# Batch 0 of a frequency filter and two-layer network on pairs of PSUM banks instead of single ones

## The chip, the cores and the metric

The kernel runs on one core of a Trainium2 chip. The metric is device time in microseconds (us) of one execution. Single executions of one kernel spread, so small differences are read in two ways: from the times of several executions, as a ratio with a 95% interval, and from milestones inside a trace of one execution.

## The reference, cut to what matters

```python
# x: 8 batches x 3008 positions x 256 channels; filters: 1505 frequencies x 256
Y = np.fft.rfft(x, axis=1) * (filt_r + 1j * filt_i)[None]
y = np.fft.irfft(Y, n=3008, axis=1).reshape(8 * 3008, 256)
h = y @ w_in                                   # 256 -> 2048
out = (0.5 * h * (1 + erf(h / sqrt(2)))) @ w_out   # 2048 -> 256
```

The two large products are 78% of the chain that ended last in the kernel before (41% and 37%). The Fourier transform is done as small products with cosine and sine tables, 3008 = 47 x 64.

## The kernel before: the parts that matter

The transforms of batches 1 to 7 run inside the slots of the main loop, beside the large products, and go through memory between their stages. Batch 0 has nothing to hide behind. It stays on the chip and alternates small products with transposes:

- `c1`: first forward stage, 8 groups, as the columns of x land; `c1t` transposes it into `b_sb`.
- `c2`: second forward stage and, on VectorE, its product with the filters `F` (real and imaginary). There are twelve of these, "products 0 to 11". The filters arrive in four transfers, and the last brings what products 8 to 11 need.
- `c3`: first inverse stage into `vt`, six copies of two halves on ScalarE.
- `c3t` and `s4`: transpose and last inverse stage into `y`, from which the first large product reads.

Everything passes through PSUM, which the kernel takes as eight banks of 512 fp32 columns. Before, each stage takes single banks in rotation:

```python
def bank(self, name, wide=False):
    pools = {"f": self.ps_f, "h": self.ps_h, "o": self.ps_o}   # 3, 3 and 2 banks
    tag = "f"
    if wide:
        tag = "fhofhofh"[self.turn % 8]
        self.turn += 1
    return pools[tag].tile([128, 512], FP32, tag=tag, name=name)

def c2(self, p):
    p1, p2 = (self.pp.tile([128, 512], BF16, tag=t, name=t) for t in ("p1", "p2"))
    for t, o, n in ((p1, 1, 0), (p2, 0, 1)):
        ps = self.bank("ps_c2", True)
        ...                                     # two matmuls of 256 columns
        nc.vector.tensor_tensor(out=t, in0=ps, op=ALU.mult, in1=F[:, n, ...])

# main part, before the loop over the large products
for u in range(16): m.c1(u // 2, u % 2)         # one half of a group each
m.tables_inverse()                              # T4, T4c and T3, before the filter stage
for p in range(14):
    if p < 12: m.c1t(p)
    if 1 <= p < 13: m.c2(p - 1)
    if p in (3, 5, 7, 9, 11, 13): m.c3((p - 3) // 2)
for u in range(20):
    if u < 16: m.c3t(u)
    if u >= 3 and u % 2 == 1 and (u - 3) // 2 < 8:
        for h in range(2): m.s4(0, (u - 3) // 2, h, both=True)
```

## Time and profile before

| | before |
|---|---|
| time, median of 4 (lowest to highest) | 791.66 us (790.64 to 792.34) |
| span of the profiled execution | 790.6 us |
| TensorE busy | 762.5 us, 96% |
| second half of product 8 starts | 35.26 us |
| last `vt` copy ends | 41.04 us |
| first w_in product | 50.20 us |
| first w_out product | 60.43 us |

Up to the first w_in product it is batch 0's own speed that counts, and from there on TensorE is busy nearly all the time (729.7 of 740.4 us). So a microsecond gained or lost before 50.2 should show at the end. In the stretch from the last `vt` copy to the first w_in product the groups by form are, on VectorE and ScalarE (name of the line, engine, operation, what it writes and reads, shapes, count, busy us and mean ns, idle before):

```profile
L218 DVE CAST d_sb<-ps_c3t 96x512 bf16<-96x512 f32 x8 | 5.3, 678 | 2.2 <-PE ps_c3t L383 2.2
...
L216 ACT ACTIVATE d_sb<-ps_c3t 96x512 bf16<-96x512 f32 x8 | 4.7, 595 | 0.4 <-PE ps_c3t L383 0.4
L220 DVE TENSOR_SCALAR y_sb<-ps_s 128x376 bf16<-128x376 f32 x8 | 4.3, 538 | 0.1
L216 ACT ACTIVATE y_sb<-ps_s 128x376 bf16<-128x376 f32 x8 | 3.9, 486 | 1.0 <-PE ps_s L306 0.8
```

Both engines copy both stages evenly and VectorE hardly idles once it has begun.

### The profile page before, as it was taken

Reading aid. Unit: us, or ns where it says so; the run is one execution under the profiler, and the core shown is the slowest. Engines: PE = TensorE matmul, PEld = TensorE weight load, DVE = VectorE, ACT = ScalarE, POOL = GpSimd, SP = SyncE. Lnnn points to the kernel's source line nnn. Section 1 sums busy time; section 2 is a strip of 40 time slices with the busy share of each in tenths; the row PEclk is TensorE's granted clock in tenths of the full one; section 3 lists DMA queues with packets and bytes.
Section 4 is the critical chain, followed back from the end, with each engine's and each line's share of the span. In section 5 each row is a group of like instructions: output and inputs, shape, how many; then the busy total and the mean of one; then the engine's idle time right before and its main releaser. Section 6 shows DMA issues by size and latency. Waiting matters only on the chain.

```text
span 790.6 us, 14618 instructions
## 1 busy us (share of the span) xinstructions
PE 762.5 (96%) x5817; PEld 539.1 (68%) x5914; DVE 407.6 (52%) x733; ACT 570.5 (72%) x982; POOL 65.3 (8%) x161
## 2 busy tenths in 40 slices
PE   4799999999999999999999999999999999999997
PEld 4556776677676767667677676667767767666666
DVE  7784756466464645646455564546645366411011
ACT  6688965798557885588755887569865688666663
POOL 8610200011000200002000010001100000000000
PEclk9999999999999999999999999999999999999999
DMA  8994862555435553446614566154642521401111
GB/s 128 178 161 132 158 161 68 147 119 114 114 84 155 104 135 84 109 139 130 145 50 109 148 119 157 40 160 108 125 130 65 162 78 58 133 31 38 41 41 54
DMA packets 88390, 87.21 MB, mean 110 GB/s; under 512 B 6081, under 2 KB 78273, under 8 KB 88321
## 3 DMA queue, kind: packets, MB, share of 16 engines
q1 hardware_dynamic: 77760, 68.70, 30.6%
q0 software_dynamic: 10560, 17.57, 15.5%
q8 instruction: 46, 0.75, 0.4%
q14 instruction: 24, 0.19, 0.1%
HBM read 57.15 MB, written 46.66 MB: 131 GB/s over the span
## 4 chain that ended last, share of the span: by engine, by line
PE 90%; DMA 5%; DVE 2%; POOL 1%; issue 1%; ACT 0%; SPq 0%; DVEq 0%; POOLq 0%
PE ps_o L420 41%; PE ps_h L406 37%; PE ps_s L231 3%; PE ps_s L306 3%; PE ps_s L278 2%; PE ps_s L254 2%; DMA d_sb<-R 1%; DMA F<-in_filt_i_dram 1%; DMA F<-in_filt_r_dram 1%; DMA x_sb<-in_x_dram 1%; DVE d_sb L218 1%; POOL x_sb L87 1%; POOL F L95 1%; DMA R<-a_sb 1%; DMA b_sb<-R 0%
## 5 line engine op out<-in xcount | busy, mean ns | idle before, releaser
L409 ACT ACTIVATE g_sb<-ps_h 128x512 bf16<-128x512 f32 x752 | 439.4, 597 | 189.1 <-PE ps_h L406 163.5
L420 PE MATMUL ps_o<-w_out_sb,g_sb 128*128 128x256 bf16 x3008 | 449.0, 272 | 3.0
L406 PE MATMUL ps_h<-y_sb,w_in_sb 128*128 128x512 bf16 (+2 forms) x1503 | 426.6, 365 | 0.2 <-ACT y_sb L216 0.2
L420 PEld LDWEIGHTS <-g_sb 128*128 128x128 bf16 x3008 | 287.6, 98 | 133.7
L406 PEld LDWEIGHTS <-w_in_sb 128*128 128x128 bf16 x1600 | 155.1, 98 | 23.0 <-issue 0.5
L424 DVE COPY ost<-ps_o 128x512 f32<-128x512 f32 x94 | 64.4, 685 | 125.1 <-PE ps_o L420 124.6
L261 DVE TENSOR_TENSOR p<-ps_s,F 128x512 bf16<-128x512 f32 x84 | 58.1, 692 | 103.8 <-ACT p L260 97.3
L220 DVE TENSOR_SCALAR y_sb<-ps_s 128x376 bf16<-128x376 f32 x120 | 65.3, 548 | 82.0 <-PE ps_s L306 81.9
L218 DVE CAST a_sb<-ps_s 96x512 bf16<-96x512 f32 x112 | 76.3, 685 | 40.5 <-PE ps_s L231 40.4
L218 DVE CAST v_sb<-ps_s 128x512 bf16<-128x512 f32 x84 | 57.6, 687 | 12.9 <-PE ps_s L278 12.7
L306 PEld LDWEIGHTS <-d_sb 96*128 96x128 bf16 x512 | 33.8, 97 | 30.2 <-issue 2.3
L259 ACT ACTIVATE p<-ps_s 64x512 bf16<-64x512 f32 x84 | 49.9, 594 | 2.2 <-ACT g_sb L409 0.2
L260 ACT CAST p<-ps_s 64x512 bf16<-64x512 f32 x84 | 48.5, 577 | 1.0
L100 POOL COPY gate<-p 1x1 bf16<-1x1 bf16 x48 | 8.5, 176 | 480.6 <-DVE p L263 480.6
L231 PE MATMUL ps_s<-x_sb,T 94*96 94x512 bf16 x112 | 42.6, 381 | 0.5
L306 PE MATMUL ps_s<-T,d_sb 96*128 96x94 bf16 x448 | 36.3, 204 | 2.6 <-DMA d_sb<-R 1.3
L263 DVE TENSOR_TENSOR p<-p,p 128x512 bf16<-128x512 bf16 x84 | 35.7, 425 | 2.9
L87 POOL DMA_DIRECT2D x_sb<-in_x_dram x64 | 33.9, 530 | 19.0 <-issue 11.1
L262 DVE TENSOR_TENSOR p<-p,F 128x512 bf16<-128x512 bf16 x84 | 34.9, 415 | 0.0
L254 PE MATMUL ps_s<-b_sb,T 128*128 128x256 bf16 x168 | 32.1, 273 | 0.3
L278 PE MATMUL ps_s<-p,T 128*128 128x256 bf16 x168 | 32.1, 273 | 0.3
L278 PEld LDWEIGHTS <-T 128*128 128x128 bf16 x168 | 16.4, 98 | 20.1 <-DVE p L263 0.5
(84 smaller groups left out, 189.0 us busy)
## 6 DMA issues: line engine op xcount, KB each, us to landing
out_dram<-ost SPq DMA_DIRECT2D x94, 256.0 KB, 2.5
x_sb<-in_x_dram POOLq DMA_DIRECT2D x64, 188.0 KB, 3.9
R<-a_sb SPq DMA_DIRECT2D x56, 192.0 KB, 3.0
b_sb<-R SPq DMA_DIRECT2D x28, 384.0 KB, 4.4
R<-v_sb SPq DMA_DIRECT2D x42, 256.0 KB, 4.0
d_sb<-R SPq DMA_DIRECT2D x56, 192.0 KB, 4.6
w_in_sb<-in_moe_w_in_dram POOLq DMA_DIRECT2D x2, 512.0 KB, 8.6
w_out_sb<-in_moe_w_out_dram POOLq DMA_DIRECT2D x2, 512.0 KB, 10.1
```

Source lines behind the costliest of these rows:

```text
L218: self.nc.vector.tensor_copy(out=out, in_=in_)
L220: self.nc.vector.tensor_scalar(out=out, in0=in_, scalar1=scale, scalar2=None, op0=ALU.mult)
L231: nc.tensor.matmul(ps[0:96, :], lhsT=self.T1, rhs=self.st[b, "x"][:, 2 * u:2 * u + 2, :], start=True, stop=True)
L259: nc.scalar.activation(out=p2[0:64], in_=ps[64:128], func=AF.Copy, scale=-1.0)
L260: nc.scalar.copy(out=p2[64:128], in_=ps[0:64])
L261: nc.vector.tensor_tensor(out=p1, in0=ps, in1=f(0), op=ALU.mult)
L278: nc.tensor.matmul(ps[:, 256 * i:256 * i + 256], lhsT=self.T3[:, k].rearrange("p a b -> p (a b)"), rhs=w[:, 256 * i:256 * i + 256], start= ...
L306: nc.tensor.matmul(ps[:, 94 * i:94 * i + 94], lhsT=d[:, (grp % 2) * 4 + i, 128 * half:128 * half + 128], rhs=t4, start=True, stop=True)
L406: nc.tensor.matmul(ps[:, o:o + n], lhsT=self.w_in_sb[:, dc, jc * 128:jc * 128 + 128], rhs=self.ring[:, dc, off:off + n], start=(dc == 0), ...
L409: nc.scalar.activation(out=self.st["g", t][:, jc, :], in_=ps, func=AF.Gelu)
L420: nc.tensor.matmul(ps[:, tile_i % 2, :], lhsT=g[:, jc, tile_i * 128:tile_i * 128 + 128], rhs=self.w_out_sb[:, jc, :], start=(jc == 0), sto ...
L424: nc.vector.tensor_copy(out=ost, in_=ps)
```

## The change

The intent: a copy or product over two banks is one instruction instead of two, so that what an instruction costs beside its columns is paid once. All of batch 0 goes to four pairs of banks, VectorE and ScalarE work on 1024 columns at once, transposes run two groups ahead of the filter stage, and the inverse tables move from in front of it into it. After batch 0 the pairs are given up and the single banks opened. Three smaller things come with it: both copies of a `c1` group now go to one engine (ScalarE for groups 0 to 3, VectorE for 4 to 7; before, groups 3 to 7 alternated), all copies of the table T3 go to ScalarE, and the load of the Gelu table moves into `c1`. The diff, cut:

```diff
-    def bank(self, name, wide=False):
-        ...
+    def pair(self, name):                      # ps_w: 4 buffers
+        return self.ps_w.tile([128, 2, 512], FP32, tag="w", name=name)
...
+    def table_4(self):
+        ps = self.pair("ps_t4")
+        for i, (t4, t1, wt) in enumerate(((self.T4, self.T1p, self.wt), (self.T4c, self.T1q, self.wtc))):
+            o = ps[0:96, i, 0:2 * NA]
+            nc.tensor.matmul(o, lhsT=t1..., rhs=self.eye..., start=True, stop=True)
+            nc.vector.tensor_scalar(out=t4..., in0=o..., scalar1=wt[0:96], scalar2=None, op0=ALU.mult)
...
     def c2(self, p):
-        for t, o, n in ((p1, 1, 0), (p2, 0, 1)):
-            ps = self.bank("ps_c2", True)
-            ...
-            nc.vector.tensor_tensor(out=t, in0=ps, op=ALU.mult, in1=self.F[:, n, ...])
+        ps = self.pair("ps_c2")
+        for t, o in ((0, 1), (1, 0)):
+            ...
+        nc.vector.tensor_tensor(out=w, in0=ps, op=ALU.mult, in1=self.F[:, :, ...])
... # c1, c1t, c3, c3t and the last stage (now c4) likewise
-    m.tables_inverse()
-    for p in range(14):
-        ...
+    m.c1t(0)
+    m.c1t(1)
+    for q in range(7):
+        if q < 6:
+            m.c2(2 * q)
+            m.c2(2 * q + 1)
+        if q % 2 == 0 and q < 6:
+            m.table_3(q // 2)
+        if q + 2 < 6:
+            m.c1t(q + 2)
+        if q == 4:
+            m.table_4()
+        if q >= 1:
+            m.c3(q - 1)
-    for u in range(20):
-        ...
+    for u in range(10):
+        if u < 8:
+            m.c3t(u)
+        if u >= 2:
+            m.c4(u - 2)
+    wide.close()
+    m.late_pools()
```

## The prediction

> **What bounds the kernel now.** I read the page's chain first, because the change touches only batch 0 and what matters is how long batch 0 lies on the path to the end. Its shares by engine and line:
>
> ```profile
> PE 90%; DMA 5%; DVE 2%; POOL 1%; issue 1%; ACT 0%; SPq 0%; DVEq 0%; POOLq 0%
> PE ps_o L420 41%; PE ps_h L406 37%; PE ps_s L231 3%; PE ps_s L306 3%; PE ps_s L278 2%; PE ps_s L254 2%; DMA d_sb<-R 1%; DMA F<-in_filt_i_dram 1%; DMA F<-in_filt_r_dram 1%; DMA x_sb<-in_x_dram 1%; DVE d_sb L218 1%; POOL x_sb L87 1%; POOL F L95 1%; DMA R<-a_sb 1%; DMA b_sb<-R 0%
> ```
>
> PE is 90% of the chain and 78% is the two large products. Batch 0 can only be the rest: transfers, and a little DVE. The chain in order of time (start, length, what) over the first 51 us shows where:
>
> ```profile
> 29.64 5.50 DMA F<-in_filt_i_dram
> 35.87 2.42 DVE p L352 x4
> 38.28 0.57 issue
> 38.86 0.69 DVE p L352
> 39.59 0.35 PE ps_c L366 x3
> 39.97 1.08 ACT vt_sb L370 x2
> 41.10 0.58 PE ps_c3t L383 x7
> 41.70 1.28 DVE d_sb L218 x2
> ...
> 49.67 0.49 ACT y_sb L216
> 50.20 0.61 PE ps_h L406 x2
> ```
>
> Up to 35.1 us the chain is the filter transfers; batch 0 only follows them. From 35.1 to 50.2 it is batch 0's work after the last filter chunk: products, last inverse (c3), then an alternation of transposes (c3t) and last stage (s4). From 50.2 on PE paces. The page's slices say PE is at 9 tenths from slice 4 to the end, so whatever moves the 50.2 moves the end by about as much. The question is only: what happens to the 15 us between the last filter's landing and the first large product?
>
> The waits of the first 62 us and the groups by form give the durations:
>
> ```profile
> DVE p L352 <- DMA F<-in_filt_i_dram: 4.1, 3, 1.9
> L352 DVE TENSOR_TENSOR p<-ps_c,F 128x512 bf16<-128x512 f32 x24 | 14.9, 684 | 5.3 <-DMA F<-in_filt_i_dram 4.1 <-DMA F<-in_filt_r_dram 0.6 <-PE ps_c L349 0.6
> L370 ACT CAST vt_sb<-ps_c 128x512 bf16<-128x512 f32 x12 | 6.4, 590 | 7.7 <-PE ps_c L366 7.7
> L199 PE MATMUL ps_t<-eye,T 128*128 128x128 bf16 x24 | 2.7, 306 | 0.2 <-ACT at_sb L216 0.2
> ```
>
> DVE stands waiting for filters three times; ACT has much idle time here. And the timeline, DVE and PE around the last landing (start, length, engine, line):
>
> ```profile
> 35.26 4.28 DVE L352 TENSOR_TENSOR p<-ps_c,F 128x512 bf16<-128x512 f32 x7 [1.87 <-DMA F<-in_filt_i_dram]
> 39.59 0.79 PE L366 MATMUL ps_c<-T,p 128*128 128x128 bf16 x11 [0.37 <-DVE p L352]
> ```
>
> Seven half products follow back to back (0.60 us from start to start), so before the change nothing but DVE lies between the landing and 39.54.
>
> [...] the two vt copies of 590 ns take 1.07 together, and 1536 elements took 1475 ns where 512 take 597, which is 0.86 ns each. [...] the 384- and 512-column evictions (546 and 685 ns) give 1.09[...]. [...] the 24 transposes of L199 took 2.66 us (111 ns each) at 15.9, the 8 of L335 at 18.39 took 0.61 (56 ns apart).
>
> **The change part by part.**
>
> *Front end, before 35 us.* The inverse tables leave the stretch 15.2 to 18.4 and 24 copies of 512 become 12 of 1024. This is all in front of the filter landing. POOL's order of loads is unchanged in the built program, and each load waits only for a load eight places earlier, so I keep 35.26 for the start of the first product with the last chunk. A new cost: a pair is tracked as one tile. In the built program the second half of each c1 pair waits for the first half's copy. That makes c1 about 1.2 us a group (0.35 + 0.55 twice, less overlap), 2.4 per x chunk against chunks that land 2.65 apart, so it fits. Following the waits through, products 5 to 7 run from 29.5 to 32.9 and c2 for products 8 and 9 is in PSUM by 32.9: 2.4 us of slack. Worth on the path: 0.
>
> *The four last products.* Eight halves, of which one (real filter) could run before 35.26, become four wholes that need both filters: 4 x 1.14 + 0.08 = 4.6 against 4.28 us. +0.3.
>
> *table_4 where it was put: the step I rest on.* PE's order is c2(8), c2(9), table_3(2), table_4 (two matmuls), c3(3), c2(10), c2(11), c3(4), c3(5). In the built program table_4's second matmul waits for DVE's copy of its first, again because the pair is one tile. On DVE that copy stands behind products 8 and 9, which need the last filter. So PE, which used to have c2 of products 8 to 10 ready ahead, stands still from about 33.6 until DVE has done both. My working, in us, with PE warm:
> - DVE: product 8 at 35.26, product 9 at 36.40, T4 copy 37.53 to 37.84 (0.31 as L193 now).
> - PE: second table matmul 37.9; 16 matmuls of c3(3) at 0.057 each, to 38.86; four of c2(10), 0.60 as the groups of L349 show, 39.46.
> - DVE: product 10 at 39.50, product 11 at 40.64 to 41.85. Without the stall it would have ended at 39.9.
> - PE: the last 12 matmuls of c3(5), 0.85, 42.75. ACT: one copy of 1024[...], to 43.8.
>
> Before, vt was complete at 41.04. So +2.75.
>
> *c3t and c4.* Before 41.04 to 50.20, 9.15 us, DVE bound: a pair of copies (0.60 + 0.46) every 1.06 us. After: the flip gives ACT seven of the eight c3t copies (0.95 each start to start) and DVE seven of eight c4 copies[...]. Steady, one c3t and one c4 of double size take 0.95 on the two engines, against 1.06 for the same work before: eight of them 7.6 against 8.5. But the pipe is coarser: fill (8 transposes, 0.65, then a 1.02 copy, then 8 matmuls) and end (last c3t copy to V + 7.6, c4(7) to 8.2, DVE copy to 9.15, where V is vt complete). The late pools make PE wait for this copy even for the first s1, which used to run before it: s1 V + 9.2, first large product V + 9.4. Against 9.15: +0.25.
>
> *PE clock.* [...] If PE is then cold, c3(3) costs 0.9 more, c2(10) 0.35, c3(5) 0.6 and the first transposes some: an estimate of 2 us from the two spacings above. [...] I give it 0.4: +0.8.
>
> *Main loop.* Same instructions in the same order; p1 and p2 now share a tile of 4 buffers, so ACT's first copy also waits for the product stage four back, over 10 us earlier. Nothing.
>
> Sum: 0 + 2.75 + 0.25 + 0.8 = +3.8 on 791.65: about 795.4.
>
> **The rivals.**
> - *It is faster, as intended:* fewer fixed costs[...] and no table stage. It would take 1 to 2 us off, 790. For it: DVE bound the alternation. Against it: the front part ends at a landing that does not move, and the tail's DVE saving is eaten by the coarser pipe.
> - *The filter landing hides everything:* only +0.3 for the products and some 0.25 after, 792.2. This is what happens if the PE stall is shorter than I think, for example if DVE takes the T4 copy earlier. The order of the built program speaks against it.
> - *Cold PE throughout the alternation:* transposes at 0.11 make 16 groups of about 0.9 us; up to +7, 798.5.[...]
>
> **Range and chances.** The terms are small against 791.65, so 2% (15.8 us) is out of reach of every rival: same is nearly sure. Within it, the stall (+2.75) is well supported and the clock term splits the result into about 794.6 and 796.6; single runs spread by 1.7. Predicted 795.4, range 793.0 to 797.8; faster 0.01, same 0.98, slower 0.01.
>
> **What would show it.** Right: the product after the last landing starts at about 35.3; PE has an idle stretch from about 33.6 to 37.9, ended by DVE's T4 copy; product 10 starts about 39.5; vt complete at 43.8 (warm) or about 45 (cold, seen in 0.11 us spacing of L358); the first gelu near 54 to 56 instead of 50.85; everything later shifted equally. Wrong: the filter landing itself moves (POOL's issues at other times), PE passes table_4 without a stall, or the alternation takes under 8.5 us from vt to the first large product.

The sum is 0 + 2.75 + 0.25 + 0.8 = 3.8 us on 791.65, so 795.4. The lengths that are used are near those that the trace of the changed kernel shows: 1.14 us from start to start of two wide products (2.35 us for both, the first 1.22; four took 4.64 in e6), 1.01 us for a `vt` copy, and 0.95 from start to start of seven `c3t` copies (6.74 us). In the 0.8 a slow clock after a stall, and the chance of 0.4, were the guess; the 2 us are an estimate from the spacings of 111 and 56 ns.

## The result, and the profile after

| | before | after |
|---|---|---|
| time, median (lowest to highest), 4 runs each | 791.66 (790.64 to 792.34) | 796.61 (795.68 to 798.29) |
| product 8 starts | 35.26 | 35.28 |
| last `vt` copy ends | 41.04 | 43.79 |
| first w_in product | 50.20 | 53.31 |
| first w_out product | 60.43 | 64.99 |
| span | 790.6 | 795.1 |

The ratio of the times is 1.0066, with an interval of 1.0045 to 1.0086. A ratio is the mean time of one kernel's runs over that of the other's of the same rounds, so it is not quite the ratio of the medians. The change costs 5 us; it is well inside 2%, so the class is "same", and not the gain it was meant for. In the two traces 4.5 us can be placed: 2.75 up to the last `vt` copy, 0.36 from there to the first w_in product (9.16 became 9.52), 1.45 from the first w_in to the first w_out product (10.23 became 11.68), and -0.06 over the remaining 730 us.

The chain that ended last, by engine, and then in order of time (start, length, what), for the kernel after:

```profile
PE 92%; DMA 3%; ACT 2%; issue 1%; DVE 1%; POOL 0%; SPq 0%; POOLq 0%; ACTq 0%
```

```profile
32.53 1.02 ACT b_sb L332
33.59 1.07 PE ps_c L358 x16
34.68 1.02 ACT vt_sb L362
35.74 0.61 PE ps_t L201 x8
36.42 1.21 DVE p L345
...
38.12 0.90 PE ps_c L358 x16
39.01 0.45 PE ps_c L342 x4
...
40.63 1.23 DVE p L345
41.90 0.86 PE ps_c L358 x12
42.78 1.02 ACT vt_sb L362
...
46.57 4.68 ACT d_sb L212 x5
51.30 0.52 PE ps_c L390 x8
51.84 0.95 DVE y_sb L216
```

Compare this with the chain of before. There it was one filter transfer up to 35.1 us, and the work followed it. Here the chain that the profile gives no longer passes through that transfer. It is a ladder of TensorE and ScalarE: a pair is filled, copied in 1.02 us, filled again. One of its steps is not a wait, though: product 9, at 36.42, doesn't read the table product that comes before it in the chain. VectorE ran it straight after product 8, and product 8 was released by the transfer. The transfer still ends at the same time (35.15 against 35.14 us), but the matmuls of product 8 have come level with it: they ended near 35.1. The timeline, VectorE and TensorE, after the landing:

```profile
35.28 2.35 DVE L345 TENSOR_TENSOR p<-ps_c,F 128x1024 bf16<-128x1024 f32 x2 [1.72 <-DMA F<-in_filt_i_dram]
...
39.49 2.36 DVE L345 TENSOR_TENSOR p<-ps_c,F 128x1024 bf16<-128x1024 f32 x2 [1.01 <-PE ps_c L342]
```

```profile
37.91 0.20 PE L193 MATMUL ps_t<-eye,T1q 94*96 94x94 bf16 x1 [1.52 <-DVE T L195]
```

Before, seven half products ran on from 35.26 to 39.54. Now two whole products run, then VectorE has nothing of them for 1.9 us, then two more run to 41.85. The third line shows TensorE standing 1.52 us until VectorE has copied the first inverse table. So from product 8 to the last `vt` copy it is 8.5 us, not 5.8. In the stretch after that, the groups by form that answer to those of before:

```profile
L212 ACT ACTIVATE d_sb<-ps_c3t 96x1024 bf16<-96x1024 f32 x7 | 6.6, 1021 | 0.8 <-PE ps_c3t L375 0.7
L216 DVE TENSOR_SCALAR y_sb<-ps_c 128x752 bf16<-128x752 f32 x7 | 6.2, 937 | 0.5 <-PE ps_c L390 0.5
...
L214 DVE CAST d_sb<-ps_c3t 96x1024 bf16<-96x1024 f32 x1 | 1.2, 1220 | 3.1 <-PE ps_c3t L375 3.1
```

The busy time did shrink: VectorE 5.3 + 4.3 = 9.6 before, 6.2 + 1.2 = 7.4 after. It did not help, because the engines begin later (3.1 against 2.2 us idle before VectorE's first copy) and because at the end the last pair must be copied whole, 0.95 us, before the first s1 and w_in product can run.

The last part is the clock. Windows of the kernel after (from and to, length, then the busy time and count of TensorE, its weight loads, VectorE, ScalarE and GpSimd, then the granted TensorE clock, the DMA share and GB/s):

```profile
52.00:53.00 1.00, 0.16 (x1) 0.14 (x2) 0.78 (x1) 0.00 (x0) 0.00 (x0) 1.00 0.22 26
53.00:54.00 1.00, 0.94 (x4) 0.46 (x4) 0.69 (x1) 0.23 (x1) 0.00 (x0) 0.81 0.00 0
54.00:55.00 1.00, 1.00 (x4) 0.36 (x3) 0.69 (x1) 0.42 (x2) 0.00 (x0) 0.50 0.00 0
...
57.00:58.00 1.00, 1.00 (x6) 0.46 (x5) 0.77 (x2) 0.60 (x1) 0.00 (x0) 0.98 0.00 0
```

and two microseconds after its first w_in product in the kernel before:

```profile
52.00:53.00 1.00, 1.00 (x6) 0.47 (x5) 1.00 (x2) 0.89 (x3) 0.00 (x0) 1.00 0.18 24
```

From about 53.6 to 57.0 us TensorE ran at half clock: four matmuls in a microsecond instead of six. That is the 1.45 us. Before, the clock stayed at 1.00.

### The profile page after: what moved, and what is told of

The parts are those of the page before. It is cut to its first block, busy times and chain, and to the rows that moved or that the text cites. A ratio compares the mean times of both kernels' runs of the same rounds, so it can differ in the third digit from the quotient of the medians.

```text
span 795.1 us, 14565 instructions
## 1 busy us (share of the span) xinstructions
PE 763.9 (96%) x5817; PEld 539.6 (68%) x5914; DVE 405.5 (51%) x713; ACT 569.8 (72%) x959; POOL 65.0 (8%) x161
## 4 chain that ended last, share of the span: by engine, by line
PE 92%; DMA 3%; ACT 2%; issue 1%; DVE 1%; POOL 0%; SPq 0%; POOLq 0%; ACTq 0%
PE ps_o L427 41%; PE ps_h L413 37%; PE ps_s L227 3%; PE ps_s L300 3%; PE ps_s L250 2%; PE ps_s L275 2%; DMA d_sb<-R 2%; ACT d_sb L212 1%; DMA x_sb<-in_x_dram 1%; DVE at_sb L214 1%; ACT vt_sb L362 1%; PE ps_c L358 0%; PE ps_c L317 0%; PE ps_c L342 0%; ACT b_sb L332 0%
## 5 line engine op out<-in xcount | busy, mean ns | idle before, releaser
L216 DVE TENSOR_SCALAR y_sb<-ps_s 128x376 bf16<-128x376 f32 x112 | 61.0, 548 | 82.1 <-PE ps_s L300 82.1
L300 PEld LDWEIGHTS <-d_sb 96*128 96x128 bf16 x448 | 30.3, 97 | 28.4 <-DMA d_sb<-R 3.4
L260 DVE TENSOR_TENSOR p<-p 128x512 bf16<-128x512 bf16 x84 | 35.7, 425 | 2.9
```

Of the source, the lines that this page charges most:

```text
L216: self.nc.vector.tensor_scalar(out=out, in0=in_, scalar1=scale, scalar2=None, op0=ALU.mult)
L300: nc.tensor.matmul(ps[:, 94 * i:94 * i + 94], lhsT=d[:, (grp % 2) * 4 + i, 128 * half:128 * half + 128], rhs=t4, start=True, stop=True)
```

## The experiments

Three reasons were on the table after the two traces. **Theory A:** `table_4` is in the wrong place; its second product waits behind products 8 and 9, and products 10 and 11 wait behind it. **Theory B:** four pairs are too few separately released buffers, so products 10 and 11 can't be made ready before the landing, whatever is done with `table_4`. **Theory C:** the half clock in the first slots of the main loop costs its own 1 to 1.5 us. Times of "before" differ by up to 0.9 us (medians 791.66, 792.03, 792.04, 792.51, 791.98; the last four on chips 4, 4, 8 and 10), so ratios are compared, not medians. All twelve kernels gave correct results.

### e1: the wait inside `table_4` taken away

```diff
+        for i in range(2):
+            nc.tensor.matmul(ps[0:96, i, 0:2 * NA], lhsT=t[i][1]..., rhs=self.eye..., start=True, stop=True)
+        for i in range(2):
+            nc.vector.tensor_scalar(out=t[i][0]..., in0=ps[0:96, i, 0:2 * NA]..., ...)
```

> Changed kernel, table_4 alone altered: both small matmuls are given to PE before the two DVE copies, so PE no longer waits inside table_4 for a copy that stands behind products 8 and 9. Theory A (as predicted: this wait is what makes the tail long): c3(3) starts about 36.5 instead of 37.95, product 10 near 38.0, vt complete near 42.3 instead of 43.8, and the time falls by about 1.5 us. Theory B (formed from the trace: the front end is late, and c3(3) needs the PSUM pair that table_3(2)'s copy frees only at 37.4): c3(3) starts at 37.45, product 10 at 39.0, vt at 43.3, only 0.5 us gained.

Measured: 798.16 us (797.08 to 799.06, 5 runs), ratio 1.0074 (1.0061 to 1.0087). Product 8 started at 35.85, the last `vt` copy ended at 45.27, 9.4 us later instead of 8.5. TensorE no longer stands at `table_4`, but:

```profile
38.18 1.05 PE L360 MATMUL ps_c<-T,p 128*128 128x128 bf16 x16 [1.01 <-ACT T L207]
40.33 1.03 PE L344 MATMUL ps_c<-b_sb,T 128*128 128x256 bf16 x8 [1.10 <-ACT vt_sb L364]
```

With the table's wait gone, TensorE waits first for the pair that `table_3` holds (ScalarE's T copy) and then, before the matmuls of products 10 and 11, for the pair of c3's copy. The pairs come free in another order. Theory A falls: the table's wait was only the one that happened to end last. Theory B's 43.3 for the last `vt` copy missed too; the pair that became free went to other work than products 10 and 11.

### e2: c1 with its eight matmuls ahead of its two copies

```diff
         for half in range(2):
             for i in range(4):
                 self.nc.tensor.matmul(ps[:, half, 96 * i:96 * i + 96], ...)
+        for half in range(2):
             self._evac(...)
```

> Changed kernel, c1 alone altered: the eight matmuls of a pair first, then its two copies, so the second half no longer waits for the first half's copy. Both theories: c1 ends about 2 us earlier than 18.9, the c2 of products 8 and 9 is in PSUM well before 35, PE then stands at table_4 from about 34 instead of 36.4, but c3(3) still starts at 37.9 to 38.0 because DVE's order and the filter landing at 35.3 have not moved: vt at 43.8, time unchanged (within 0.4 us). If the front end itself were on the path, the time would fall by 0.5 us or more.

Measured: 796.66 us (795.93 to 797.46, 5 runs), ratio 1.0059 (1.0047 to 1.0071). Product 8 started at 34.90, again released by the filters, and the last `vt` copy came 8.5 us later, as in the changed kernel. A quicker front end by itself is worth nothing that these runs can tell.

### e3: dummy products that keep TensorE busy around the last c4

```diff
+        if u == 7:
+            self.fill(ps[:, 0, :], 4)      # 4 matmuls of 128x512, overwritten by c4
...
+    m.fill(m.pair("ps_fill")[:, 0, :], 5)  # 5 more, never read
     wide.close()
```

> Changed kernel plus nine dummy 128x512 matmuls on PE (four before the last c4, five after it), whose results nobody reads, in stretches where PE stands idle just before the main loop. Theory C (the half clock at 53.4 to 57.0 comes of PE's low use between 50 and 53): no stretch with granted clock 0.5 after 50 us, the first 16 slots take 0.65 us each, first w_out product about 10.4 us after the first w_in product instead of 11.85, time down by 1 to 1.7 us, runs within 1 us of each other instead of 2.6. Rival (the half clock was set by the stall at 36 to 38, or by chance): the half clock stays and the time does not move.

Measured: 797.63 us (796.19 to 798.38, 5 runs), ratio 1.0069 (1.0057 to 1.0081). The granted clock reads 1.00 in each microsecond from 49 to 56, and first w_in to first w_out product took 10.21 us, as in the kernel before:

```profile
54.00:55.00 1.00, 1.00 (x6) 0.47 (x5) 0.87 (x2) 0.39 (x1) 0.00 (x0) 1.00 0.00 0
```

So Theory C has the mechanism, but the time did not fall. In the trace, 1.47 us were won there, 0.44 lost to a later product 8 (35.72), 0.18 lost to the dummies, and 2.1 lost after the first w_out product, where TensorE waits 3.3 us for the round trips of later batches through memory, all between 150 and 590 us (1.6 in the changed kernel, 1.3 before). See e11 for the same.

### e5: e1 and e2 together

> The edits of the first two runs together. Theory B: c2(10) now waits only for product 8's PSUM pair; product 10 can start behind product 9 and the two table_4 copies, near 38.1, product 11 ends at 40.4, vt at 42.3 to 42.4: 1.4 us gained against the changed kernel, more than the sum of the two alone (0.5 and 0). Theory A: the same 1.5 us as the first run alone.

Measured: 797.24 us (794.94 to 798.49, 6 runs), ratio 1.0065 (1.0052 to 1.0079). In the profiled execution product 8 started early, at 33.68, and the last `vt` copy ended at 43.10: 9.4 us, as in e1. Theory B had the last copy at 42.3; a miss, for the reason seen in e1.

### e6: e5, with both kinds of inverse table earlier

```diff
-        if q % 2 == 0 and q < 6:
-            m.table_3(q // 2)
+        if q in (0, 2, 3):
+            m.table_3({0: 0, 2: 1, 3: 2}[q])
...
-        if q == 4:
+        if q == 1:
             m.table_4()
```

> Changed kernel with c1 and table_4 as in the run that had both edits, table_4 moved two groups of products earlier and table_3(2) one group earlier, so that nothing stands between c2(9) and c2(11) but c3(3), and the c2 of products 8 to 11 can all be in PSUM at about the filter landing. Theory B (the tail is long because c2(10) and c2(11) come after the landing, for whichever wait holds them up): DVE does products 8 to 11 back to back, 4.6 us from the landing at 33.7 to 35.3; vt complete 6.5 us after the landing instead of 8.5; time down by 1.5 to 2 us against the changed kernel, to about 794.8. Rival: another wait takes its place as in the last two runs, and vt stays at 43 or later.

Measured: 797.03 us (796.32 to 798.92, 4 runs), ratio 1.0068 (1.0055 to 1.0081). Theory B had 794.8; its rival, another wait in the old one's place, has the result. VectorE:

```profile
37.95 4.64 DVE L348 TENSOR_TENSOR p<-ps_c,F 128x1024 bf16<-128x1024 f32 x4 [3.27 <-PE ps_c L345]
```

Products 8 to 11 now run back to back, in the 4.64 us of Theory B, and the last `vt` copy comes 6.6 us after product 8, not 8.5. Yet product 8 starts 2.7 us later, at 37.95, and it waits for TensorE, not for the filters. TensorE in turn waited for ScalarE's copies, twice for over a microsecond between 33 and 37 us; this is the second time:

```profile
36.42 1.05 PE L361 MATMUL ps_c<-T,p 128*128 128x128 bf16 x16 [1.16 <-ACT b_sb L335]
```

And one thing no theory had: TensorE ran at half clock in the middle of the filter stage, after 3.41 us in which it had been busy for 1.30 (the granted clock is the last number but two):

```profile
24.20:27.61 3.41, 1.30 (x19) 1.12 (x18) 2.81 (x4) 2.00 (x2) 2.96 (x6) 1.00 1.11 158
27.61:31.02 3.41, 3.41 (x29) 3.04 (x27) 2.36 (x2) 1.05 (x2) 2.98 (x6) 0.50 1.11 152
```

The last filter had landed at 34.82, so product 8 came 3.0 us later than the filters allowed. An estimate of the half clock's part, from the same groups at full clock in this trace: 1.69, 1.06, 1.06 and 1.27 us instead of 1.03, 0.61, 0.61 and 1.05, which is up to 1.8 of the 3.0 us. What is left, 1.2 us or more, is waits for pairs. So what was saved behind the landing came back in front of it, in part as half clock. It fits that there are only four pairs for the same work wherever the table's pair is held, but what this order is worth at full clock is not shown. In this trace the first slots of the main loop ran at full clock (9.99 us to the first w_out product), though the last two stages are as wide as in the changed kernel.

### e4: of the change only its last two stages

The kernel before, with c3t and c4 on pairs and everything else on single banks.

> One part of the change alone: the kernel before with only its last alternation (c3t and the last stage) on pairs of banks with 1024- and 752-column copies; products, c1 to c3 and tables as before. If the parts add up as the two traces say: vt complete at 41.0 as before, first w_in product 9.5 us later (before: 9.16), a stretch of half clock after it (first w_out product 11.7 us after the first w_in product instead of 10.2), so time up by about 0.4 to 1.9 us on the kernel before. Rival (the change's intent: fewer, larger copies are a gain where copies bound): down by 0.5 us or more.

Measured: 793.69 us (792.99 to 794.44, 4 runs), ratio 1.0021 (1.0007 to 1.0036). That is 0.0021 x 792 = 1.7 us. Product 8 to the last `vt` copy is 5.8 us, as before; from there to the first w_in product 9.97; to the first w_out product 11.19, with the clock at 0.50 from about 49.3 to 52.7 us. This part of the change costs by itself, in a kernel whose filter stage was not touched.

### e12: the change without its last two stages

The changed kernel, with c3t and s4 put back on single banks.

> The complement: the changed kernel with only the last two stages of batch 0 (from the last vt copy on) put back on single banks as before. If the parts add up, the last vt copy stays at 43.8 (43.5 to 44.3), from there to the first w_in product is 9.2 (9.1 to 9.4, against 9.52), from the first w_in to the first w_out product 10.2 (10.2 to 10.6, against 11.68), and the time is 796.6 - 1.65 = 795.0 (794.5 to 795.4), 2.7 to 3.3 over the kernel before. If the half clock comes from the stall at the inverse table at 36 to 38 us and not from the wide last stages, the stretch to the first w_out product stays at 11 to 11.7 and the time at 796 to 797.

Measured: 796.41 us (795.23 to 798.14, 5 runs), ratio 1.0048 (1.0036 to 1.0061), which is 3.8 us. The milestones came as expected: last `vt` copy 43.86, first w_in product 9.28 us later, first w_out product another 10.25, clock 1.00 throughout the profiled execution. The time did not: 794.5 to 795.4 was expected, and 796.41 lies in the rival's range, though "before" was slower in that call too. The span was 793.4, so 2.8 us more than before, while the mean of the runs says 3.8; 2.8 lies just below its interval (2.85 to 4.83). Of e4 and e12 the costs add to 5.5 us, and the whole change cost 5.2. In these traces the half clock of the first slots goes with the wide last stages and not with the stall at `table_4`, which is in this kernel unchanged. Wide last stages don't always bring it, as e6 shows. One more thing is to be seen in this trace:

```profile
35.35 2.35 DVE L355 TENSOR_TENSOR p<-ps_c,F 128x1024 bf16<-128x1024 f32 x2 [1.56 <-PE ps_c L352]
```

The front end is the same as in the changed kernel, and here product 8 was released by TensorE, not by the filters, which had landed at 35.07. Where they land earlier the front end alone decides. In e3, with the same front end, they had landed at 33.93:

```profile
35.72 2.36 DVE L345 TENSOR_TENSOR p<-ps_c,F 128x1024 bf16<-128x1024 f32 x2 [1.56 <-PE ps_c L342]
```

In e1 it was 34.13 and 35.85. In e4 and e11, which have the front end of the kernel before, product 8 followed the landings (34.39 and 34.24) within 0.13 us. So in these traces an early landing helps the front end of the kernel before and not that of the changed one. And where no filter held it up, product 8 started 3.92 us after product 6 in e1, e3, e5 and e12, against 2.76 us with single banks in e10.

### e11: e4 with the dummy products

> The kernel before with only the last two stages of batch 0 on pairs (which alone cost 1.65 us, 793.69 against 792.04), plus the nine dummy 128x512 products around the last one. Theory C (of its 1.65 us, about 1 is the half clock of TensorE in the first slots of the main loop: first w_in to first w_out product 11.19 us against 10.23): that stretch falls to 10.2 to 10.3, granted clock 1.00 in each microsecond after the first w_in product, time 792.5 to 793.0. Rival (the half clock is filled by other waits, or the fill delays the first w_in product by as much): the stretch falls but the time stays at 793.4 to 794.2.

Measured: 793.53 us (792.96 to 794.4, 5 runs), ratio 1.0009 (0.9996 to 1.0023). The clock stayed at 1.00 and first w_in to first w_out product took 10.23 us. The ratio is 0.0012 lower than that of e4, so about 1 us, as Theory C has it, but the intervals overlap, and the time of 793.53 lies in the rival's range of its own expectation because "before" was slower in that call too. So: agrees, not proven. As in e3, the stretch after the first w_out product was long (732.5 us against 730.6 in e4), with the same 3.3 us of waits for round trips of later batches. Why dummies at 50 us should lengthen waits at 150 us and later stays open.

### e8 and e9: half the filter bytes from memory

Two of the four copies of each filter chunk are made from the chip's own memory, so that the last chunk might land earlier; e8 does it to the kernel before, e9 to the changed one.

```diff
-            for q, a in enumerate((direct, mirror, direct, mirror)):
+            for q, a in enumerate((direct, mirror)):
                 nc.gpsimd.dma_start(out=self.F[32 * q:32 * q + 32, ...], in_=a)
+            nc.sync.dma_start(out=self.F[64:128, ...], in_=self.F[0:64, ...])
```

> The kernel before with half the filter bytes from HBM: partitions 64 to 127 of F, which equal 0 to 63, are copied from there by transfers inside SBUF (16 loads instead of 32, and 8 copies on the SP queue). If the filter landing is what bounds batch 0 (both theories say so for the kernel before): the last filter chunk is there by about 28 us, DVE's waits for filters (5 us in the kernel before) mostly go, vt complete at 36 to 37.5 instead of 41.0, time down by 3.5 to 4.5 us, to about 788. If not: no change, or slower by the extra copies.

> The changed kernel with the same halved filter loads. If the changed kernel is slow only because it reacts slowly to the filter landing, it gains as much as the kernel before does, 4 us or more, to about 792. Theory B (its front end, four pairs and half-clock PE, is itself almost as late as the landing: c2(8) was in PSUM only at 35.1 against the landing at 35.3): products 8 and 9 start at most 0.5 us earlier, and the time falls by under 1 us, so that the distance to the kernel before with the same loads grows to about 8 us.

Measured, e8: 792.16 us (791.28 to 793.81, 4 runs), ratio 1.0009 (0.9995 to 1.0024). The second half of product 8 started at 34.13, only 1.1 us earlier, and the span was 1.1 us shorter. The rounds show no gain, so the expected 788 was a miss. The larger of the extra copies took 6.5 to 7.3 us to land, and the loads of w_in and of batch 1 now ran beside them. e9: 797.49 us (796.33 to 798.61, 4 runs), ratio 1.0070 (1.0057 to 1.0083), product 8 at 35.63 and the last `vt` copy 8.5 us later. Nothing was won, but not for Theory B's reason: the last filter copy landed at 35.51, no earlier than in the changed kernel (35.15), and product 8 waited for it.

```profile
35.63 2.36 DVE L346 TENSOR_TENSOR p<-ps_c,F 128x1024 bf16<-128x1024 f32 x2 [1.33 <-DMA F<-F]
```

So e9 tests neither theory. Its distance to e8 is 5.3 us, not the 8 that Theory B had.

### e10: e8 with the later loads held back

```diff
+        if p == 6:
+            m.gate(m.st[0, "p", p - 1][0][0:1, 0:1])   # GpSimd waits for product 5
+            m.load_w_in()
+            m.load_x(1)
+            m.load_w_out(0)
+            m.load_w_out(8)
```

> The kernel before with half the filter bytes from memory (as in the run that did only that, where the last filter landed 1.1 us earlier and the time stayed) and with the loads of w_in, of batch 1 and of w_out held back on GpSimd until product 5 is done (near 27 us), so that the filters' transfers have the queues for themselves. Theory P (the filter landing is what the stage up to the first w_in product waits for, and these loads took from it): VectorE no longer waits for filters (2.8 us in the run with half the bytes, 5 us in the kernel before); product 8 starts at 31.5 to 33, the last vt copy ends at 37 to 38.5 against 41.0, the first w_in product at 46 to 48 against 50.2, time 788.5 to 790 against 792. Rival Q (what is held back comes too late): the filters land early but w_in, or batch 1's columns, land after they are wanted; the first w_in product or the first s1 waits for DMA, time 791 to 795. Rival R (the filters' landing is bound by their own copies, not by the other loads): product 8 stays at 34, time 792.

Measured: 791.49 us (790.24 to 793.36, 5 runs), ratio 0.9987 (0.9974 to 1.0001). In the view of the waits VectorE no longer waits for filters. It waits for TensorE, and TensorE for ScalarE's copies:

```profile
DVE p L353 <- PE ps_c L350: 2.9, 6, 0.8
...
PE ps_c L350 <- ACT b_sb L340: 1.8, 5, 0.6
```

Two of VectorE's waits are for filters all the same: 0.85 us to 22.35 and 0.26 us to 25.09 both end 0.12 us after a filter copy landed, long after the matmuls of these products. From product 3 on none is left. The second half of product 8 started near 33.5 (two halves into a row of four that began at 31.70, at 0.6 each, is product 8's first half at 32.9), the last `vt` copy ended at 39.66 and the first w_in product came at 48.83. So the landing was the bound of the kernel before, but with the rest only 1.4 us behind it. Theory P was right on the landing and wrong on its worth. 791.49 is the lowest median of all runs, with an interval that just reaches 1; it is not shown to beat the kernel before.

### e13: e10 with wide products alone

Here c2 takes two pairs and the other stages of that part four single banks; all eight are single again for c3t and s4. It is the idea of the change, tried where the filters do not hide it.

```diff
+        w = self.pp.tile([128, 2, 512], BF16, tag="p12", name="p12")
+        ps = self.ps_w.tile([128, 2, 512], FP32, tag="w", name="ps_c2")     # 2 pairs
...
+        nc.vector.tensor_tensor(out=w, in0=ps, op=ALU.mult, in1=self.F[:, :, ...])
```

> The run with half the filter bytes and the later loads held back (filters landed early; there the 24 products of 512 columns ran from 20.8 to 38.2 us, 15.6 us of work and 1.7 of waits for TensorE; last vt copy 39.7; ratio 0.9987), with one more edit: the products alone take 1024 columns at once from two double banks, everything else stays on single banks (four in that stage, eight again after it). Theory W (with the landing out of the way VectorE's products bound the stage, so the wide product is worth its 24 x 0.65 - 12 x 1.20 = 1.2 us): products end near 37.0, last vt copy at 38.2 to 38.8, ratio 0.996 to 0.998 (789.5 to 791 against 792.5). Rival T (two pairs and four single banks are too few: TensorE, which has 13 us of products in the same stage, waits for a VectorE or ScalarE copy at each product): VectorE waits for TensorE over 3 us in the stage, products end at 38.5 to 40, ratio 0.999 to 1.001. Rival V (the stage's time is passed on only in part, as with half the filter bytes alone, where 1.1 us in the trace gave 0.1 in the rounds): the products end early but the ratio stays at 0.998 to 1.000.

Measured: 792.38 us (791.29 to 792.91, 5 runs), ratio 1.0000 (0.9986 to 1.0014). Product groups of e10 and then of e13, both on VectorE:

```profile
L353 DVE TENSOR_TENSOR p<-ps_c,F 128x512 bf16<-128x512 f32 x24 | 15.0, 684 | 3.1 <-PE ps_c L350 2.9 <-PE ps_c L367 0.3
```

```profile
L363 DVE TENSOR_TENSOR p<-ps_c,F 128x1024 bf16<-128x1024 f32 x12 | 14.2, 1221 | 5.1 <-PE ps_c1t L346 1.9 <-PE ps_c L360 1.7 <-DMA F<-in_filt_i_dram 1.5
```

The wide products save 0.8 us of VectorE's time and bring 2.0 us of waits. Products ended at 38.66, with a ratio of 1.0000, both as rival T has it, but not for its reason. The view puts 3.6 us down to TensorE, and the longest of these waits is misnamed: product 2 started at 25.16, 0.12 us after a filter copy landed (25.04), and its matmuls had been done at 22.8. The 1.5 us put down to the filters are product 0's, whose matmuls ended at 20.8 just before it started at 20.89. After product 0 TensorE kept VectorE waiting for 1.7 us, not for over 3. A wide product needs both filters, where in e10 the real half of product 2 ran ahead of the imaginary filter. From the start of product 0 to the end of product 11 it was 17.8 us, 17.4 in e10: no gain. What no theory had was a half-clock stretch, from 40.3 to 43.7 us, after TensorE had been busy for only 1.6 of 3.4 us around the last wide product. The 16 transposes at 40.27 took 1.85 us instead of 1.01, and from the last `vt` copy to the first w_in product it was 10.26 us. So the ratio of 1.0000 is not that of the wide products alone.

### All runs beside each other

| run | product 8 | to last `vt` copy | to first w_in | to first w_out | to the end | ratio |
|---|---|---|---|---|---|---|
| before | 35.26 | 5.8 | 9.16 | 10.23 | 730.2 | 1 |
| after | 35.28 | 8.5 | 9.52 | 11.68 | 730.1 | 1.0066 |
| e1, table_4 free | 35.85 | 9.4 | 9.53 | 11.68 | 730.5 | 1.0074 |
| e2, c1 quicker | 34.90 | 8.5 | 9.52 | 11.67 | 730.8 | 1.0059 |
| e3, dummies | 35.72 | 8.5 | 9.70 | 10.21 | 732.2 | 1.0069 |
| e5, e1 + e2 | 33.68 | 9.4 | 9.79 | 11.40 | 730.2 | 1.0065 |
| e6, tables earlier | 37.95 | 6.6 | 9.52 | 9.99 | 731.0 | 1.0068 |
| e9, after, half filters | 35.63 | 8.5 | 9.63 | 11.57 | 731.2 | 1.0070 |
| e12, narrow last stages | 35.35 | 8.5 | 9.28 | 10.25 | 730.0 | 1.0048 |
| e4, wide last stages only | 34.52 | 5.8 | 9.97 | 11.19 | 730.6 | 1.0021 |
| e11, e4 + dummies | 34.36 | 5.8 | 9.73 | 10.23 | 732.5 | 1.0009 |
| e8, before, half filters | 34.13 | 5.8 | 9.17 | 10.24 | 730.2 | 1.0009 |
| e10, e8 + loads held back | 33.5 | 6.2 | 9.17 | 10.23 | 730.6 | 0.9987 |
| e13, e10 + wide products | 33.1 | 7.1 | 10.26 | 10.23 | 730.4 | 1.0000 |

All columns but the ratio come from one profiled execution each, in us; "product 8" is its start, or that of its second half where it has two. The landing alone moves by more than a microsecond between executions: with the same loads, the last filter landed at 32.77 in e5 and at 35.15 in the changed kernel. The distances are steadier. Product 8 to the last `vt` copy is 5.8 us for single banks (6.2 in e10, where no filter holds it up), 8.5 for the change, 9.4 with `table_4` freed and 6.6 with the tables earlier, in each run of the kind.

## Why the prediction was right or wrong

It said 795.4 us, range 793.0 to 797.8; it was 796.61, in the range and 1.2 us above the point. Its rival of a gain fell, that of a landing that hides everything (792.2) too, and that of a cold TensorE throughout the alternation (798.5): the clock was 1.00 there.

*Front end, worth 0 on the path.* Product 8 started at 35.28 against the predicted 35.26. Right in the number, but by luck: the working under it was wrong. "2.4 us of slack" were about 0.2, and only because the landing was late (35.15) in that execution. In e1, e3 and e12, with the same front end, TensorE and not the landing released product 8, in e1 and e3 1.7 and 1.8 us after it. The step that failed is "c1 about 1.2 us a group": a half took 0.48 us for its four matmuls and waited for the other half's copy (0.58 to 0.79 us of idle time before each run of eight matmuls from 10.13 us on), so c1 took 1.6 us a group (matmuls of groups start at 13.02, 14.61, 16.20 and 17.79). TensorE also stayed at half speed longer: the first clock record of the traces, to full speed, is at 18.36 us before and at 22.90 after, and 15 of c1t's transposes at 18.92 took 1.78 us, 0.11 us each, where the kernel before had reached 0.056 by 18.39. (The view of windows reads a clock of 1.00 before the first record too, from 15 to 18 us in the kernel before, where 24 transposes took 2.66 us, 0.11 each. It is a default of the view, for the trace holds no earlier record.)

*Four last products +0.3, and table_4, together +2.75 to the last `vt` copy.* Measured +2.75, and the steps to the tenth: product 10 at 39.49 (predicted 39.50), product 11 done at 41.85 (41.85), `vt` at 43.79 (43.8), TensorE's second table product at 37.91 (37.9). Only the stall was shorter, 1.52 us and not 4.3: it began at 36.4 and not at 33.6, because TensorE came later. But the reason that the prediction rested on, the place of `table_4`, is only half of it. It was true as a description of which wait ends last. As a cause it fails: "without the stall it would have ended at 39.9" is refuted by e1, where the stall was gone and product 11 ended at 43.33. What the runs point to in its place is the number of pairs. e1, e5 and e6 each move the wait to another pair; none shortens the path up to the last `vt` copy except by an earlier landing. This is argued from the waits and not isolated: no run changed the number of pairs alone, the copies grew with them (1.02 us for 0.59), and e6 lost time to the half clock as well.

*c3t and c4, +0.25.* Measured +0.36 in the pair of traces, from 9.52 against 9.16. e4 had more, 9.97, part of it from the half clock that fell at 49.3 into this stretch already. The mechanism given, a coarser pipe that eats the saving in busy time, is what the groups show: 2.2 us less VectorE time and no earlier end.

*Clock, +0.8.* This is the term that was misplaced. The prediction looked for a cold TensorE after the stall at 36 us, with a chance of 0.4 and 2 us if it came. The clock held at 1.00 there in the traces of the changed kernel, e2, e3 and e12, which have the stall. It fell instead in the first slots of the main loop, after the wide last stages had left TensorE busy for 1.91 of the 3.41 us before it, with no gap over 1.03 us, and it cost 1.45 us. The trace of e12 (stall kept, last stages narrow) has no half clock; that of e4 (no stall, last stages wide) has it; in those of e3 and e11 the dummies remove it; in that of e6, with wide last stages, it fell elsewhere. Nor does it come in every execution: the mean granted clocks of the changed kernel's four are 0.997, 0.999, 0.995 and 0.999, and one such stretch takes 1.7 of 795 us, or 0.002. So, as an estimate from these means, two of them (796.26 and 795.68 us) had none, against 796.95 and 798.29 for the others. That a chance of one half times 1.45 us is near the 0.8 put down is luck. For the profiled execution, with 1.45 in place of 0.8 the sum is 2.75 + 0.36 + 1.45 = 4.56, against 4.5 in the spans.

What makes the clock fall is not shown. It fell after TensorE had been busy for 2.05 of 3.40 us in e4, for 1.61 of 3.40 in e13 and for 1.30 of 3.41 in e6. It held through 35 to 38 us in the changed kernel with 1.25 of 3.00. In the 3 us up to 53 in the changed kernel and up to 54 in e6, each time just before the first w_in product, TensorE was busy for 1.56 in both; then the clock fell in the changed kernel and held in e6. So the busy share alone does not decide it. The half-clock stretch was 3.4 us long in each of the eight traces that show one (after, e1, e2, e4, e5, e6, e9, e13).

*Main loop, nothing.* Right for the change: -0.06 in the traces. Not for the runs with dummies, which stays open.

Also open: the times differ by about half a microsecond more than the traces account for (4.95 by medians, 4.5 by spans). Single runs of the changed kernel differ by 2.6 us, so one trace can't settle that. The late landing of the profiled execution, which hid the slower front end, is a candidate.

Why does the wider instruction save so little in the first place? Seven half products took 4.28 us, so one costs 0.60 us from start to start, two of them 1.20. A wide one costs 1.14 (two took 2.35, the first 1.22). Back to back, 0.06 us is all that is left to save. Twelve such savings are 0.7 us; the waits that came with the pairs were larger in each kernel that used them in the filter stage.

## What to carry to other kernels

Count the buffers that are released separately, not the bytes: joining two banks into one tracked tile halves the number of independent slots and lengthens each turn (here a copy of 1.02 us for one of 0.59), and here it came with waits longer than the 0.06 us that it saved an instruction. A trace in which a transfer lands late (35.15 us in the changed kernel) hides a slow stage in front of it; look at executions in which it lands early too (33.93 in e3, where product 8 started only at 35.72). The wait that ends last in a trace is not yet a cause; take it away before you say what it is worth, for others may stand behind it (1.52 us at `table_4`; without it, waits of 1.01 and 1.10 us in e1). And look past the stretch that you change: a TensorE that was left half busy before a dense loop (1.56 of 3 us) began that loop at half clock in the changed kernel, which cost 1.45 us, and at full clock in e6.
